# One planned kernel, planned anew: a lower rate for GpSimd's one-tile operations beside VectorE

## The chip, the core and the metric

The kernel runs on one core of a Trainium2 chip. A core has five engines that work side by side, each through its own list of instructions, in order: TensorE (PE in the profile; its weight loads are PEld), VectorE (DVE), ScalarE (ACT), GpSimd (POOL) and SyncE (SP), which here only starts transfers. They meet at semaphores. Tiles lie in SBUF, matmul results in the eight banks of PSUM. The metric is the device time of one execution in microseconds (us), and the median of several executions is compared.

## The reference, cut to what matters

```python
def _attn_ref(q, k, v, n_global, n_local):      # q, k, v: 4 x 8 heads x 768 x 64
    scores = scale * np.matmul(q, k.transpose(0, 1, 3, 2))
    keep = is_global | is_local                 # 8 first keys, and 96 keys back
    scores = np.where(keep, scores + bias, -1000000000.0)
    a = np.exp(scores - np.max(scores, axis=-1, keepdims=True))
    return np.matmul(a / (np.sum(a, axis=-1, keepdims=True) + 1e-09), v)

def _moe_ref(x, w_in, g_ln, w_sg, b_sg, w_out): # x: 4 x 768 x 512
    h = gelu(x @ w_in)
    u, v = h[..., :512], h[..., 512:]
    v_n = (v - mu) / np.sqrt(var + 1e-06) * g_ln
    v_s = np.einsum('ts,bsd->btd', w_sg, v_n) + b_sg[None, :, None]
    return x + (u * v_s) @ w_out
```

The output of the attention, heads side by side, is the x of the second part.

## The kernel before

**The work.** The attention is cut into 48 units, one for each of 4 batches, 3 pairs of query tiles (u) and 4 pairs of heads (j). A unit loads qk and v, makes its scores on PE (`score`, tile s_ps, L1049), and goes through `softmax`: DVE adds the bias and finds the row extreme (four instructions p, pst <- s_ps, L1071), ACT takes the exponential and its row sum (L1076), a tiny addition to the sums follows (pst, L1083 on ACT, L1085 on POOL or L1087 on DVE), DVE takes the reciprocal (L1089), and four instructions multiply p by it (L1096 on POOL, L1094 on ACT, L1099 on DVE). The first 16 units may do this last step on POOL alone; the later ones on POOL, ACT or DVE. These multiplications read one tile and write it: they are the "one-tile operations" of this document, called POOL_TS in the code. Then p is transposed: for the first 16 units on PE (`turn_full`, tps, L1157, copied to pt by ACT or DVE at L1162 and L1163), for the others by DVE in 32x32 blocks (tt, L1125) and two transfers through DRAM (far, L1133, and pt, L1137; `turn_blocks`). PE multiplies pt with v (av, L1184), and the result goes to x as a high and a low part (xh L1282, x L1294 to L1300 for the first units, L1257 and L1261 for the later ones).

The second part runs batch by batch, one batch behind the attention, on fp32 data split into a high and a low part, so that each product is three matmuls (mm_ps, L556 to L558): `v_tile` (then gelu and normalisation, then the split into z, L588 and L592), `u_tile`, `mix_tile` (y, L646 and L649, split into gt) and `out_tile` (o, L670 and L672). The last batch's last product is done in blocks (class `Blocks`, L801, with its sums at L747 and splits at L720 and L723). The weights arrive as 64-bit floats, are put together from their two words by one ACT and three DVE instructions (stage, L877 to L884) and are split too (win, wsg, wout, L887 to L889), all of this in the first third of the run.

**What sets the order.** No order is written by hand. `Plan.op` collects every operation with the engines it may run on, each with a busy time and an end, and `Plan.order` then plays the whole program forward on a model of the engines: at each step an engine takes the first operation that is ready, has its buffers and has the smallest key. The key is a due time, counted back from PE's list in `Plan.due`, plus a shift of the operation's own, read from the table `SHIFTS` (two digits for each operation). Three numbers in `RULES` say when an operation waits for a faster engine (`calm_at`), how early a load may start (`early`) and what a place on DVE is worth (`price`). The table is the result of a search made elsewhere, and `emit` writes the instructions in the order that comes out, so each engine's list is fixed before the kernel runs.

In that model an SBUF operation on DVE ("DVE_SB") and a two-tile operation on POOL ("POOL", such as a product or a difference of two tiles) keep out of each other's way: `begin` lets neither start before the other has ended (`held`). `emit` holds the POOL one to it with a wait on DVE (L524 and following). One-tile operations of POOL take part in none of this: `on_pool_ts` (L190) counts 0.05 + n/390 us for n columns, whatever DVE does meanwhile.

Where the model sees PE idle for over 0.6 us before 29 us, `keep_on` fills the gap with matmuls of zeros (`bsg` as both inputs, L505), so that the clock of PE stays up. How many is worked out from the gap in `zeros`. They are executed whatever the gap turns out to be.

Of the kernel before, what the change touches and what calls it, by code (L numbers as in the profile page):

```python
# [1652 lines left out]
```

## Time and profile before

| what | value |
|---|---|
| runs | 413.01, 413.61, 416.01 us; median 413.61 us |
| the profiled execution | 415.03 us, of which 413.3 us from its first to its last instruction (the span) |
| granted clock of PE | 0.998 of full speed |
| DVE, ACT and POOL instructions that the profile counts | 1032, 764 and 382 |

The profile's first table gives the busy time of each engine; a busy PE is one whose matmuls follow each other closely. In the tables of stretches each engine has its busy microseconds in that stretch and, in brackets, its instructions. In a timeline each row has a start, a length, the engine, the line of the kernel, the operation, output<-input, how many such instructions follow each other, and, in square brackets, how long the engine was idle before them and who ended that. In the tables of waits a row says who waited at which line for whom, then the total in us, how often, and the longest.

### The profile page before, as it was taken

The page shows a single profiled execution, that of the slowest core. Times are in us where ns is not written, and L with a number is a line of the kernel's source. Part 1 is how long each engine was busy: PE and PEld are TensorE (multiplying, and loading weights), DVE is VectorE, ACT ScalarE, POOL GpSimd, SP SyncE. Part 2 cuts the span into 40 slices and gives each one's busy share as a digit, 9 for nine tenths or more (in the row PEclk, how much of TensorE's full clock was granted, in tenths as well). Part 3 has the DMA queues.
Part 4 walks back from the last instruction along what each step waited for, and adds up shares of the span by engine and source line. Part 5 has one row for each costly group of instructions (what it writes and reads, how often), then busy time and mean ns, then how long its engine had stood idle before and what let it go on. Part 6 is the DMA issues. An engine that isn't in the chain of part 4 may idle for free.

```text
span 413.3 us, 11290 instructions
## 1 busy us (share of the span) xinstructions
PE 399.9 (97%) x3980; PEld 359.7 (87%) x3980; DVE 323.3 (78%) x1032; ACT 233.6 (57%) x764; POOL 231.3 (56%) x382
## 2 busy tenths in 40 slices
PE   8879989999999999999999999999999999999995
PEld 4667768899987888999999888989999888999994
DVE  6886899999887898986667699977667587734883
ACT  5889999776756574654155555844155233523510
POOL 3776888875954455454354156364354033899650
PEclk9999999999999999999999999999999999999999
DMA  7847665447779687757586586736575531000003
GB/s 237 311 150 228 215 214 177 132 118 252 217 248 299 205 238 217 199 150 219 165 256 178 166 281 173 227 89 214 162 235 144 149 120 38 1 2 0 2 17 143
DMA packets 50031, 70.15 MB, mean 170 GB/s; under 512 B 5808, under 2 KB 33968, under 8 KB 49968
## 3 DMA queue, kind: packets, MB, share of 16 engines
q1 hardware_dynamic: 49968, 69.36, 54.9%
q8 instruction: 33, 0.54, 0.5%
q14 instruction: 30, 0.25, 0.2%
HBM read 50.99 MB, written 18.35 MB: 168 GB/s over the span
## 4 chain that ended last, share of the span: by engine, by line
PE 59%; DVE 16%; DMA 9%; ACT 6%; SPq 3%; POOL 3%; issue 3%; DVEq 0%; POOLq 0%
PE mm_ps L556 15%; PE mm_ps L558 14%; PE mm_ps L557 14%; PE av L1184 5%; DMA pt<-far 5%; PE s_ps L1049 5%; PE mm_ps L801 4%; DMA far<-tt 3%; SPq L1133 3%; ACT p L1076 2%; POOL p L1096 2%; DVE tt L1125 2%; DVE p L1071 2%; PE tps L1157 2%; DVE z L592 1%
## 5 line engine op out<-in xcount | busy, mean ns | idle before, releaser
L1096 POOL TENSOR_SCALAR p<-p,pst 128x192 f32<-128x192 f32 (+1 forms) x179 | 90.9, 526 | 27.7 <-DVE pst L1089 24.1
L1076 ACT ACTIVATE p<-p,pst 128x192 f32<-128x192 f32 (+1 forms) x192 | 84.2, 444 | 31.4 <-DVE pst L1071 31.3
L556 PE MATMUL mm_ps<-wsg,z 128*128 128x384 f32 x192 | 65.0, 339 | 0.1
L557 PE MATMUL mm_ps<-wsg,z 128*128 128x384 f32 x192 | 64.3, 335 | 0.3 <-DVE wsg L889 0.3
L558 PE MATMUL mm_ps<-wsg,z 128*128 128x384 f32 x192 | 64.4, 336 | 0.1
L1071 DVE CUSTOM_DVE_ANT_0 p<-s_ps,bias 128x192 f32<-128x192 f32 (+1 forms) x192 | 57.1, 339 | 5.9 <-PE s_ps L1049 4.0
L1184 PEld LDWEIGHTS av<-pt,v 64*64 64x64 f32 x1408 | 41.1, 133 | 9.9 <-issue 4.1
L1184 PE MATMUL av<-pt,v 64*64 64x128 f32 (+1 forms) x1408 | 48.5, 250 | 1.2 <-DMA pt<-far 1.1
L672 POOL TENSOR_TENSOR o<-o,x 128x384 f32<-128x384 f32 x24 | 24.6, 1027 | 40.9 <-DVE o L670 21.4
L556 PE MATMUL mm_ps<-x,win 128*128 128x384 f32 x128 | 44.0, 343 | 0.0
L558 PE MATMUL mm_ps<-x,win 128*128 128x384 f32 x128 | 42.9, 335 | 0.0
L557 PE MATMUL mm_ps<-x,win 128*128 128x384 f32 x128 | 42.8, 335 | 0.0
L1049 PE MATMUL s_ps<-qk 64*64 64x192 f32 (+1 forms) x768 | 41.4, 320 | 0.0
L556 PE MATMUL mm_ps<-win,x 128*128 128x512 f32 x96 | 39.8, 415 | 0.0
L558 PE MATMUL mm_ps<-win,x 128*128 128x512 f32 x96 | 37.7, 393 | 0.0
L557 PE MATMUL mm_ps<-win,x 128*128 128x512 f32 x96 | 37.6, 392 | 0.0
L1125 DVE STREAM_TRANSPOSE tt<-p 128x384 f32<-128x384 f32 (+1 forms) x64 | 33.0, 542 | 5.8 <-DMA far<-tt 4.5
L556 PEld LDWEIGHTS mm_ps<-wsg,z 128*128 128x128 f32 x192 | 36.0, 188 | 1.6 <-issue 1.0
L1076 ACT ACTIVATION_READ_ACCUMULATOR p<-p,pst 128x1 f32 x192 | 37.2, 194 | 0.0
L558 PEld LDWEIGHTS mm_ps<-wsg,z 128*128 128x128 f32 x192 | 36.0, 188 | 0.8 <-DVE z L592 0.7
L557 PEld LDWEIGHTS mm_ps<-wsg,z 128*128 128x128 f32 x192 | 36.0, 188 | 0.6 <-DVE wsg L889 0.6
L1085 POOL TENSOR_SCALAR pst<-pst 128x4 f32<-128x4 f32 x39 | 9.5, 245 | 45.9 <-ACT p L1076 36.7
(130 smaller groups left out, 931.3 us busy)
## 6 DMA issues: line engine op xcount, KB each, us to landing
qk<-in_qk_in_dram SPq DMA_DIRECT2D x32, 416.0 KB, 4.2
far<-tt SPq DMA_DIRECT2D x96, 96.0 KB, 3.0
pt<-far SPq DMA_DIRECT2D x24, 384.0 KB, 4.7
v<-in_v_in_dram SPq DMA_DIRECT2D x32, 256.0 KB, 3.9
out_dram<-o SPq DMA_DIRECT2D x32, 192.0 KB, 2.2
qk<-in_qk_in_dram SPq DMA_DIRECT2D x16, 288.0 KB, 3.9
v<-in_v_in_dram SPq DMA_DIRECT2D x16, 192.0 KB, 3.1
far<-tt SPq DMA_DIRECT2D x32, 80.0 KB, 2.5
```

Of the source, the lines that this page charges most:

```text
L556: mm(ps.ap, ah, bh, start=(i == 0), stop=False)
L557: mm(ps.ap, ah, bl, start=False, stop=False)
L558: mm(ps.ap, al, bh, start=False, stop=(i == n - 1))
L672: lo = lambda eng: eng.tensor_tensor(o.ap, o.ap, xm[:, 1, :].bitcast(F32), ALU.add)
L801: mm(ps.ap, pa(h)[:, ms], pb(g), start=(first and k == n == 0), stop=True, skip_group_check=True)
L1049: nc.tensor.matmul(to, qk[rows, qc:qc + HQ], keys, start=True, stop=True)
L1071: nc.vector.tensor_tensor_reduce(out=p[:, g, 0:nk], in0=s_ps[h][:, i * W:i * W + nk], in1=bias[:, 2 * j + h, w0:w0 + nk], op0=ALU.add, op1 ...
L1076: op([on_act(nk, 0.225) + (lambda p=p, g=g, nk=nk, i=i: nc.scalar.activation(p[:, g, 0:nk], p[:, g, 0:nk], AF.Exp, bias=st[:, 0, i, g:g + ...
L1096: op([on_pool_ts(nk, -0.10) + (partial(scaled, lambda o, a, c: nc.gpsimd.tensor_scalar(o, a, c, 1.0, ALU.mult, ALU.mult)),),][:1 if n < TU ...
L1125: nc.vector.transpose(out, src.rearrange("p g (b j) -> p g b j", j=QB))
L1133: nc.sync.dma_start(far[:, :, a, 0:nt * QB].rearrange("b j f -> j b f"), tt[a * QB:(a + 1) * QB, :, 0:nt * QB])
L1184: nc.tensor.matmul(to, v[rows, vc:vc + D], of, stop=True, skip_group_check=True, **kw)
```

## The change

The model gets a rate for one-tile operations of POOL beside SBUF operations of DVE. Such an operation is counted as lengthened by 0.52 us for each us that DVE is still busy with SBUF operations, up to 1/(1 - 0.52) of its length; if DVE starts one while POOL is at work, what is left of POOL's operation is lengthened after the fact, with the operations and buffers that wait for it. PE's transposes are counted as 0.105 us for each 128 columns instead of 0.11. The search is made again on this model, so the three numbers of `RULES` and the whole table are new.

```diff
-RULES = (11.346722742318088, 16.818843568250852, 0.2893491302086273)
+RULES = (7.773165816547267, 15.003852384881524, 0.25509251116156784)
 SHIFTS = (
-    "Txi8VrTSOERgRRRKSLTBYGSjQYWsSpUpRBTgRPTfUlVPUDRPbKJ5V4YeT7YpSPS0XaNOVlSXS2c4ZEVlZVVHNVYISoRxZTTBPFOf"
...
+    "PrTKTwRJU3QHTgU5ULTpX8QFVATPSxORQsPgVgTyS2VOUuTkRrRuT6QgW6TpUiV9RTQVRURdReSISLUJUBWOT2Q1SMOCVPQARaVb"
...
-TURN = 0.11
+TURN = 0.105
...
+SLOWED = 0.52
...
-        self.ways = [(w[0].split("_")[0], w[1], w[2], w[0] in ("DVE_SB", "POOL"), w[-1])
-                     for w in ways]
+        self.ways = [(w[0].split("_")[0], w[1], w[2], w[0] in ("DVE_SB", "POOL"),
+                      w[0] == "POOL_TS", w[-1]) for w in ways]
...
+def beside(work, held):
+
+    return min(work / (1.0 - SLOWED), work + SLOWED * held) if held > 0.0 else work
...
+                if way[4]:
+                    more = beside(way[1], held["DVE"] - o.begin) - way[1]
+                    slowed = o
+                elif way[3] and e == "DVE" and slowed and free["POOL"] > o.begin:
+                    left = free["POOL"] - o.begin
+                    later = beside(left, way[1]) - left
+                    free["POOL"] += later
+                    slowed.end += later
+                    for x in slowed.after:
+                        x.ready = max(x.ready, slowed.end + SYNC)
...
                 if way[3]:
                     held[e] = free[e]
+                if e == "POOL" and not way[4]:
+                    slowed = None
```

The 24 lines that this adds shift all later lines by up to 24 (L1096 becomes L1120). No instruction that computes is added or removed; some change their engine, and the order changes on all five. The table of what changed place, counted over the lists of the two programs (the general path, which does not run, is alike in both):

| operation | engine before: count | after |
|---|---|---|
| z low part (L592) | DVE 19, POOL 5 | DVE 12, POOL 12 |
| y times u (L649) | DVE 17, POOL 15 | DVE 11, POOL 21 |
| gt low part (L592, L723) | DVE 18, POOL 12 | DVE 14, POOL 16 |
| win and wout low parts, 256 columns (L889) | DVE 1, POOL 15 | DVE 7, POOL 9 |
| p times 1/sum (L1094 to L1099) | ACT 9, DVE 4, POOL 179 | ACT 4, DVE 1, POOL 187 |
| sums + tiny (L1083 to L1087) | ACT 8, DVE 1, POOL 39 | ACT 5, DVE 3, POOL 40 |
| z high part (L588) | ACT 18, DVE 6 | ACT 21, DVE 3 |
| matmuls of zeros (L505) | 96, in runs of 12, 13, 9, 10, 8, 28, 16 | 104, in runs of 12, 15, 7, 10, 21, 25, 12, 2 |

PE changes between the small matmuls of the attention (64x64, L1049 and L1184) and full ones; it has 44 runs of small ones before and 42 now.

Three places are shown, with buffer numbers (a number is a buffer's own and differs between the two programs).

First ACT, at the fifth unit, whose softmax tiles are p_378, p_397 and pst_379 before and p_389, p_394 and pst_390 now; tps are the transposes of the units ahead of it. Before:

```order
L1076 ACTIVATE p_378,pst_379<-p_378,pst_379 128x192
L1076 ACTIVATE p_397,pst_379<-p_397,pst_379 128x192 x2
L1162 COPY pt_442<-tps_405 128x256
L877 ACTIVATE stage_447<-stage_293 128x512
L1076 ACTIVATE p_378,pst_379<-p_378,pst_379 128x192
L1282 COPY xh_463<-av_418 128x128
L1083 ACTIVATE pst_379<-pst_379,small_58 128x4
L1162 COPY pt_442<-tps_454 128x384
```

Now:

```order
L1100 ACTIVATE p_389,pst_390<-p_389,pst_390 128x192
L1100 ACTIVATE p_394,pst_390<-p_394,pst_390 128x192
L1100 ACTIVATE p_389,pst_390<-p_389,pst_390 128x192
L1100 ACTIVATE p_394,pst_390<-p_394,pst_390 128x192
L1107 ACTIVATE pst_390<-pst_390,small_58 128x4
L901 ACTIVATE stage_460<-stage_287 128x512
L1306 COPY xh_468<-av_426 128x128
L1306 COPY xh_468<-av_403 128x128
```

The four exponentials of the unit now follow each other, and its sums; before, a copy out of PSUM that waits for PE and a step on a weight stood ahead of the fourth.

Second DVE, from the same unit's reciprocal on, which is what POOL's four multiplications wait for (ISA with p is L1071's operation, s_ps is in PSUM). Before:

```order
L1089 RECIPROCAL pst_379<-pst_379 128x4
L1071 ISA p_466,pst_460<-s_ps_431,bias_87 128x192
L1071 ISA pst_460 128x1
L882 SCALAR_TENSOR_TENSOR stage_447<-stage_293,stage_447 128x512
L888 CAST win_310<-stage_371 128x512
L884 SCALAR_TENSOR_TENSOR stage_447<-stage_293,stage_447 128x512
L880 TENSOR_SCALAR stage_480<-stage_480 128x512
L882 SCALAR_TENSOR_TENSOR stage_480<-stage_381,stage_480 128x512
L1300 TENSOR_TENSOR x_478<-xh_463,x_478 128x256
L884 SCALAR_TENSOR_TENSOR stage_480<-stage_381,stage_480 128x512
L889 TENSOR_TENSOR win_310<-stage_447,win_310 128x512
```

Now:

```order
L1113 RECIPROCAL pst_390<-pst_390 128x4
L1324 TENSOR_TENSOR x_449<-xh_377,x_449 128x256
L904 TENSOR_SCALAR stage_460<-stage_460 128x512
L1095 ISA p_480,pst_481<-s_ps_442,bias_87 128x192
L1095 ISA pst_481 128x1
L1095 ISA p_486,pst_481<-s_ps_442,bias_87 128x192
L1095 ISA pst_481 128x1
L906 SCALAR_TENSOR_TENSOR stage_460<-stage_287,stage_460 128x512
L1095 ISA p_486,pst_481<-s_ps_439,bias_87 128x192
```

Before, eight operations of DVE on SBUF follow close behind the reciprocal, one behind the other; now operations that read s_ps in PSUM stand between them.

Third POOL, at the thirteenth unit, the first of the second batch (p_1077, p_1068, pst_1069 before, p_1075, p_1088, pst_1076 now). Before:

```order
L592 TENSOR_TENSOR z_1126<-vg_950,z_1126 128x512
L1300 TENSOR_TENSOR x_880<-xh_1141,x_880 128x256
L617 TENSOR_TENSOR rs_1193<-rs_1193,small_58 128x1
L1096 TENSOR_SCALAR p_1077<-p_1077,pst_1069 128x128
L1096 TENSOR_SCALAR p_1068<-p_1068,pst_1069 128x192 x2
L1096 TENSOR_SCALAR p_1077<-p_1077,pst_1069 128x128
L1096 TENSOR_SCALAR p_1164<-p_1164,pst_1152 128x128 x2
L1096 TENSOR_SCALAR p_1151<-p_1151,pst_1152 128x192 x2
```

Now:

```order
L616 TENSOR_TENSOR z_1120<-vg_933,z_1120 128x512
L1120 TENSOR_SCALAR p_1075<-p_1075,pst_1076 128x192
L1120 TENSOR_SCALAR p_1088<-p_1088,pst_1076 128x128
L1120 TENSOR_SCALAR p_1075<-p_1075,pst_1076 128x192
L1120 TENSOR_SCALAR p_1088<-p_1088,pst_1076 128x128
L1324 TENSOR_TENSOR x_888<-xh_1151,x_888 128x256
L641 TENSOR_TENSOR rs_1186<-rs_1186,small_58 128x1
L1324 TENSOR_TENSOR x_930<-xh_1236,x_930 128x256
L1120 TENSOR_SCALAR p_1159<-p_1159,pst_1160 128x192 x2
L1120 TENSOR_SCALAR p_1176<-p_1176,pst_1160 128x128 x2
```

The unit's four multiplications now stand ahead of the low part of x and of the normalisation's power (rs), behind which they stood.

More of the change, by code (lines that the diff above doesn't have):

```diff
@@ new lines @@
+    "UCU9R7R4TWVeNCTkZSStScU5TQSbWtVNTiSkQ7UARhOjNxWDX3PZK5ahWlazP5SsZwXQAWSoTHYLTJabLlS0S3UEWSR3YiORV1S9"
+    "RNSrUNTeSFRsUBRsTXTbSkRkRRPTRzRuWNQ4PwODVwQHTZVlULWgQrUqQqPJIcSWQmSETsSITgVfPoTHV2T5W2V5WwSnTASAPFT0"
+    "T9TISXOqShXyVRTOUbNxXTRUOySUMyQif4OZEVUcRXV8TDP6POSuSqOZaKU8PcVyUjWBZDUAUpO2TQTgRiNoSLVHSgIVS5VFWNWg"
+    "WOISCDGbM5CXUagEbHVtWXUoMyUobgaaQnJCTDUWSUN6WQS8VmOkRHP7U2VobpMzT0JDTXTmQLUSOXe6YkR2NDZnMdW5acSIalUj"
+    "XHNrWMV1SaUSbqN7SpQmHxXdOUcoRWLZTyRpTaQzUcSOLQggPZZ5aJT4jgPcHXPmO2PJSoMDPHZIaNCgduHHP0OnW2kbhJHzKZSW"
@@ new lines @@
+    "MNU5WOLILMWoVxVDOPZcTMOlWNMzHLWYSaWQQBN357TOK6iQNrPiEOUeaFU5RhcKMWOsPxVKcUVsUmROGRRfaIbQQgUxLnGKRBWP"
+    "UgaQYvWybiOjVZJBMITeX6HkcHTMRBYpXKJdQrQWXMWVWkPMX5LpSgToX3TtTdKactWvKIQzMXOaV9SdTYNFSNXwaHTXOIe3XAQt"
+    "dHTqVJSuTSP0IwWPOxOoTPcGfgZvO3e5NcSwXMThRfUrZVWITIQqTJTtMdWaT3TvWzYXPeXWNBT4SIWgKVa9Q8UkU9UCQdKwWJTk"
+    "SaTWSXOXO4W8ctbMYiRvQyTtRdK8ZHRNWVXzYkT8D0ZIUZPVZbTnS4TBX1ahTNQKQQO1TqlxTZXPNmTRQLSlLCYPXnXbRlY9WcOp"
+    "T1XhUDV9YrTiRoKkTgT4TaSAMvVCW4beYCMpJnUNTOVVNLXzL7QKOMQ4LZOkQnSGTohjX9XbS2Z5Z4NyUlUxO6XDo9ORdHOSV6R7"
@@ L105 @@
+    "VzS5P8VPRQUCKqSROlS8RdQAPVVCQASuVVS2PzQUVQNxatQORJUmMJQZQAQwZuV8RkUBQUUqVRV3ZcZ3S0M6PcTLRuMlRdNTMKSw"
+    "PVQqVEVKPeVzSkYUR4Q2U8YXRbRIUITJVAX7YSTxQuUrWHRcWySQSwS4Y9SLXZSAV6S0W6RDNwUEVlVEU1YLRHNvRXSWTLSSQlPl"
+    "QxWnXYRaQQ"
 )
@@ L362, in order @@
         wire, mode = 0.0, False
-        fetch, holder = Fetch(), {}
+        fetch, holder, slowed = Fetch(), {}, None
         held = {"DVE": 0.0, "POOL": 0.0}
@@ L455, in order @@
                     more += fetch.run(o.begin + more, o.words + 0.3, way[1], wire)
+                if way[4]:
[8 more added lines that the diff above has]
+                        x.ready = max(x.ready, slowed.end + SYNC)
+                    for b in slowed.bufs:
+                        if (b.kind and holder.get((b.kind, b.slot)) is b and
+                                places[b.kind][b.slot] is not None):
+                            places[b.kind][b.slot] = max(x.end for x in b.ops)
                 free[e] = o.begin + way[1] + more
```

91 lines of the change are left out of this document (39 added, 52 removed).

## The prediction

> **What bounds the kernel now.** The page's first two lines come first: of five engines one has next to no idle time.
>
> ```profile
> span 413.3 us, 11290 instructions
> PE 399.9 (97%) x3980; PEld 359.7 (87%) x3980; DVE 323.3 (78%) x1032; ACT 233.6 (57%) x764; POOL 231.3 (56%) x382
> ```
>
> PE leaves 413.3 - 399.9 = 13.4 us, and its work is the same before and after, so a plan can gain only there, in the matmuls of zeros, which count as busy, and in changes between small and full matmuls. Where that time lies, the table of stretches shows (I set the borders at the ends of PE's gaps; after the length come PE, PEld, DVE, ACT and POOL).
>
> ```profile
> 0.00:30.50 30.50, 25.47 (x378) 17.77 (x378) 24.23 (x101) 23.34 (x84) 19.26 (x44) 1.00 0.71 236
> 30.50:57.00 26.50, 26.41 (x429) 20.83 (x423) 21.73 (x99) 26.19 (x101) 19.21 (x40) 1.00 0.73 228
> 57.00:62.20 5.20, 3.64 (x23) 2.63 (x21) 4.98 (x20) 4.99 (x17) 5.20 (x10) 1.00 0.42 143
> 62.20:104.00 41.80, 41.67 (x357) 38.05 (x356) 41.15 (x127) 32.51 (x105) 31.52 (x46) 1.00 0.55 173
> 104.00:129.50 25.50, 24.33 (x261) 21.35 (x259) 21.23 (x72) 16.37 (x56) 17.82 (x32) 1.00 0.80 251
> 129.50:162.00 32.50, 32.18 (x368) 27.66 (x372) 28.42 (x102) 21.39 (x79) 15.43 (x28) 1.00 0.79 236
> 162.00:337.00 175.00, 174.90 (x1791) 162.47 (x1787) 133.97 (x429) 83.60 (x278) 77.78 (x143) 1.00 0.63 186
> 337.00:408.40 71.40, 71.29 (x409) 68.92 (x397) 47.10 (x93) 25.19 (x49) 45.12 (x45) 1.00 0.07 26
> 408.40:413.20 4.80, 0.00 (x0) 0.00 (x0) 0.49 (x1) 0.00 (x0) 0.00 (x0) 0.81 0.26 95
> ```
>
> From 162 to 408.4 us PE lacks 0.2 us: nothing can be gained there, only lost. The last 4.8 us are one addition and a store, in the same order now. The rest is 5.0 us in the first 30.5 (1.2 of them before the first instruction), 1.6 around the thirteenth unit, 1.2 between 104 and 129.5, and 0.3 after that. Second reading of the same table: ACT is full from 30.5 to 62.2 (26.19 of 26.50), DVE from 57 to 104 (41.15 of 41.80). So what PE gains early, these two have to follow.
>
> The waits say on whom PE was idle. The first two rows are of the whole span; the third is the first one's share up to 30.5 us.
>
> ```profile
> PE tps L1157 <- POOL p L1096: 5.3, 5, 1.6
> PE av L1184 <- DMA pt<-far: 1.1, 3, 0.5
> ...
> PE tps L1157 <- POOL p L1096: 3.7, 4, 1.5
> ```
>
> The largest wait of PE, 5.3 us, is for just the operations whose rate the change corrects. Is the rate wrong? POOL's groups kept apart by shape, the first up to 62.2 us, the second from 160 us on:
>
> ```profile
> L1096 POOL TENSOR_SCALAR p<-p,pst 128x192 f32<-128x192 f32 x44 | 25.6, 598 | 5.8 <-DVE pst L1089 3.2 <-DVE xh L1283 1.5 <-PE tps L1157 0.6
> ...
> L1096 POOL TENSOR_SCALAR p<-p,pst 128x192 f32<-128x192 f32 x73 | 33.2, 473 | 15.3 <-DVE pst L1089 15.1
> ```
>
> The code counts 0.442 us for 192 columns; late in the run they take 473 ns, early 598. The early ones run beside the weight operations:
>
> ```profile
> 22.90 0.69 DVE L882 SCALAR_TENSOR_TENSOR stage<-stage 128x512 int32<-128x512 int32 x1
> 22.92 4.73 POOL L1096 TENSOR_SCALAR p<-p,pst 128x192 f32<-128x192 f32 x4 [2.43 <-DVE pst L1089]
> 26.76 0.68 DVE L889 TENSOR_TENSOR win<-stage,win 128x512 fp32r<-128x512 f32 x1
> 57.66 4.64 POOL L1096 TENSOR_SCALAR p<-p,pst 128x128 f32<-128x128 f32 x8
> ```
>
> Four at 22.92 us take 4.73 us, 1.18 each, while DVE runs eight SBUF operations on end (the first and last are shown); eight at 57.66, of 128 and of 192 columns (the row names the first's shape), take 4.64, 0.58 each. PE's waits stand right behind:
>
> ```profile
> 26.36 0.55 PE L1157 MATMUL tps<-ident,p 128*128 128x128 f32 x3 [1.46 <-POOL p L1096]
> 27.70 0.55 PE L1157 MATMUL tps<-ident,p 128*128 128x128 f32 x3 [0.80 <-POOL p L1096]
> 60.67 0.66 PE L1157 MATMUL tps<-ident,p 128*128 128x128 f32 x4 [1.56 <-POOL p L1096]
> ```
>
> **The change, term by term.** *Fifth unit.* Its chain before starts on ACT and DVE:
>
> ```profile
> L908 ACT ACT_TABLE_LOAD x1 | 1.3, 1283 | 0.7 <-PEq L1639 0.7
> ...
> 5.82 0.83 ACT L1010 ACTIVATE bias<-dist 128x320 bf16<-128x320 bf16 x2 [3.59 <-DVE dist L988]
> ...
> 20.00 0.37 ACT L1162 COPY pt<-tps 128x256 f32<-128x256 f32 x1 [0.69 <-PE tps L1157]
> 20.96 0.67 ACT L877 ACTIVATE stage<-stage 128x512 f32<-128x512 f32 x1 [0.59 <-PE av L1184]
> 21.53 0.45 ACT L1076 ACTIVATE p<-p,pst 128x192 f32<-128x192 f32 x1
> 22.56 0.17 DVE L1089 RECIPROCAL pst<-pst 128x4 f32<-128x4 f32 x1
> ```
>
> The fourth exponential at 21.53 stood behind a copy and a weight step that together waited 1.3 us for PE. In the new order the four follow each other, so it can start when ACT fell idle, at 20.00 - 0.69 = 19.3; with the same 1.0 us from there to the reciprocal that is 20.3 instead of 22.56, 2.2 earlier. POOL's four then stand beside alternating PSUM and SBUF work of DVE: between 4 x 0.473 = 1.9 us and 4.73; I take 2.6, nearer the free end, since about half of DVE's time there reads PSUM. So p is ready some 2.2 + 2.1 = 4 us earlier, and the waits of 1.46 and 0.80 go. What is late next is ACT. Of the 51.2 us from 5.8 to 57 it is busy 23.34 + 26.19 - 1.5 (its table and one small instruction before) = 48.0, so it idles some 3, and its list up to the thirteenth unit shortens by 1.1 us (the groups' means over both lists). So the 3.7 us of PE's waits on POOL are not all to be had.
>
> *Zeros.* These are executed in any case:
>
> ```profile
> 7.12 2.29 PE L505 MATMUL tps<-bsg 128*128 128x384 bf16 x13
> 17.26 1.04 PE L505 MATMUL tps<-bsg 128*128 128x256 bf16 x8
> 21.69 1.73 PE L505 MATMUL av<-bsg 128*128 128x128 bf16 x28
> ```
>
> Without the drain of the last one (0.2 to 0.3 us) that is 0.16 us for each of 384 columns, 0.11 for 256, 0.055 for 128. Now there are 2 more of the first kind, 8 fewer of the second, 12 more of the third, and 2 of 512 columns (0.22 each, an estimate from these): 0.32 - 0.87 + 0.66 + 0.44 = +0.55 us. Up to the first full products I therefore have -3.7 + 0.55 = -3.15 at best, 0 at worst (ACT gives nothing back), and take -2.8: the end that ACT's 3 us of idle time allow.
>
> *Thirteenth unit.* Its multiplications started at 57.66 behind a power (0.55) and x's low part (0.73, mean 734 ns of three), both now behind them; 1.56 us of PE's wait against 0.55 + 0.73 of passed work. Between 0 and -1.6; I take -1.2. The two operations that fall behind are needed by a normalisation and by products several us later.
>
> *Changes between small and full matmuls.* 44 runs become 42.
>
> ```profile
> 54.71 0.39 PE L557 MATMUL mm_ps<-win,x 128*128 128x512 f32 x1
> 54.94 0.39 PE L558 MATMUL mm_ps<-win,x 128*128 128x512 f32 x1
> 55.26 0.70 PE L1184 MATMUL av<-pt,v 64*64 64x128 f32 x24
> ```
>
> From full to small the step is 0.32 us where it is 0.23 otherwise: 0.1 each way, so 2 x 0.2 = -0.4, between 0 and -0.8 if each change also costs a wait.
>
> *DVE to POOL.* Seven low parts of z, six products y and four low parts of gt move to POOL; six low parts of 256 columns go the other way.
>
> ```profile
> L592 POOL TENSOR_TENSOR z<-vg,z 128x512 fp32r<-128x512 f32 x5 | 6.4, 1287 | 3.6 <-DVE z L588 2.3 <-ACT z L588 1.3
> L592 DVE TENSOR_TENSOR z<-vg,z 128x512 fp32r<-128x512 f32 x19 | 13.4, 705 | 0.6
> ...
> L649 POOL TENSOR_TENSOR y<-y,u 128x384 f32<-128x384 f32 x15 | 15.1, 1018 | 9.1 <-DVE y L646 5.8 <-DVE pst L1089 1.9 <-POOL p L1096 1.2
> L649 DVE TENSOR_TENSOR y<-y,u 128x384 f32<-128x384 f32 x17 | 10.5, 620 | 0.4
> ```
>
> Each is 0.58 (z) or 0.40 (y; gt as y by my estimate) later done: 7 x 0.58 + 10 x 0.40 = 8.1 us of lateness. I cost it at nothing, because most stand after 160 us, where POOL is busy 77.78 of 175 us, PE lacks 0.1, and the last low parts of a batch's z are mostly on DVE in both lists. If that cover fails, it is up to 8.1. Of each two-tile operation on POOL, `emit` also adds a wait on DVE; behind it queue the next multiplications by 1/sum, and behind those the transposes: by DMA in that part, which POOL's idle 97 us cover. The Trainium skill speaks against this move: its GPSIMD Engine Reference, section 4.1, Engine selection, has elementwise work of two inputs belong on VectorE, about 2x slower on GpSimd. The rows agree, with 1287 against 705 ns and 1018 against 620; by that rule alone the move would be a loss of 8.1 us, by the rows of idle time it is free.
>
> *104 to 162 us.* The 1.2 and 0.3 us are waits for transfers and late tiles. The new list of PE has more full products ahead of the first units transposed by DMA, but DVE's list up to the 24th unit sums to the same 143.1 us (groups' means), and DVE was full up to 104. A PE that comes 4 us earlier may wait here: between -1.2 and +2.5; I take +0.6.
>
> The sum: -2.8 - 1.2 - 0.4 + 0 + 0.6 = -3.8 us. The profiled execution took 415.03 us, with 413.3 of span and 1.7 around it; it should become 411.2, with a span of 409.5. It lies 1.4 above the median of the runs shown, 413.61, as single runs here do (413.01 to 416.01), so the median goes to 409.8.
>
> **The rivals.**
>
> *It is given back to ACT and DVE.* For it: both are full in turn from 30.5 to 104 us, and DVE's work ahead of that point doesn't shrink. Against it: DVE idled 4.8 us between 30.5 and 57 because ACT held it, and ACT's list gets shorter. PE then waits for DVE's, ACT's or the transfers' tiles what it saved up to the first products: -3.8 + 2.8 = -1.0, so 412.6.
>
> *Everything is recovered.* If PE also loses the 1.2 and 0.3 us after 104 and pays nothing there, and ACT's 1.1 us count in full: -3.15 - 1.6 - 0.8 - 1.5 = -7, so 406.5. Against it: it takes an ACT without idle time.
>
> *Slower: POOL's two-tile work comes onto PE's path.* With the 8.1 us on the path and the other terms as forecast, 409.8 + 8.1 = 417.9; it ends above the time of before as soon as 3.8 of the 8.1 us, about half of the moved tiles, are waited for. For it: PE has no slack of its own after 162 us, and each two-tile operation also holds off DVE's next SBUF operation or is slowed by it. Against it: PE's list of waits over the whole span has four rows, and none names a two-tile operation of POOL. The rule of the Trainium skill's GPSIMD Engine Reference, section 4.1, Engine selection, would lead here.
>
> *The plan does not change what it is meant to.* The matmuls' order after 160 us keeps its grouping; if the early waits on POOL stay as they are, since the new rate is still off, the time is 413.6 plus 0.55 less 0.4: 413.8. I count it with the first rival.
>
> **How the numbers follow.** Forecast, with 407.5 to 412: 0.50. Given back or unchanged, 412 to 415: 0.26. Everything recovered, 404.5 to 407.5: 0.14. Slower, 415 to 421: 0.10. The range that leaves out 2 in 10: from 406.0, which keeps most of the recovered case, to 414.8, which keeps the second. One per cent, about what a measurement here can tell from no change, is 4.1 us: faster means under 409.5. That holds all of the recovered case and 0.24 of the forecast's 0.50, so 0.38; slower means over 417.7, somewhat over half of the last case, 0.06; the rest, 0.56, lies within.
>
> **What would show it.** Right: PE's row of waits for POOL's p under 2 us instead of 5.3; the mean of the 192-column multiplications up to 60 us nearer 500 than 598 ns; PE's first full product of win and x some 2.5 us earlier; the stretch from 162 us on unchanged in length. Given back: the same, but new rows of PE's waits for DVE, ACT or pt<-far of over 3 us between 57 and 162. Slower: PE idle after 162 us, with POOL's z, y or gt as the releaser. The forecast is wrong as a whole if PE's waits for POOL shrink and the first stage doesn't.

## The result, and the profile after

The changed kernel takes 412.84 us in the median (411.45 to 414.68, 22 runs). The kernel before, run beside it on the same chip, takes 415.27 us (413.01 to 416.82, 22 runs), so the ratio is 0.9941 with an interval of 0.9927 to 0.9955: 0.6 per cent faster, 2.4 us. The first three runs of before, with their median of 413.61 us, lay at the low side of what this kernel does; against those three the gain would look like 0.8 us. The profiled execution took 413.24 us, with a span of 411.5.

The page of the changed kernel, its span and the busy time of each engine:

```profile
span 411.5 us, 11298 instructions
PE 399.2 (97%) x3987; PEld 361.1 (88%) x3988; DVE 312.9 (76%) x1024; ACT 231.8 (56%) x749; POOL 245.5 (60%) x405
```

10.4 us moved from DVE's busy time, and 14.2 us came to POOL's: the two-tile operations that changed engine. PE now lacks 12.3 us of its span instead of 13.4. The table of stretches of the changed kernel, with the same borders (length, then PE, PEld, DVE, ACT, POOL, granted clock, DMA share, GB/s):

```profile
0.00:30.50 30.50, 27.48 (x393) 20.22 (x395) 24.50 (x104) 24.71 (x90) 17.63 (x47) 1.00 0.77 249
30.50:57.00 26.50, 26.50 (x425) 20.97 (x424) 21.66 (x98) 25.54 (x95) 20.53 (x44) 1.00 0.68 212
57.00:62.20 5.20, 4.31 (x56) 3.32 (x55) 5.13 (x20) 5.10 (x18) 3.82 (x7) 1.00 0.45 157
62.20:104.00 41.80, 39.67 (x310) 36.01 (x309) 40.50 (x126) 31.57 (x100) 28.89 (x43) 1.00 0.52 161
104.00:129.50 25.50, 25.50 (x274) 23.58 (x273) 22.02 (x77) 15.47 (x54) 17.34 (x31) 1.00 0.87 265
129.50:162.00 32.50, 32.40 (x374) 27.13 (x373) 27.52 (x98) 20.46 (x72) 21.15 (x37) 1.00 0.76 223
162.00:337.00 175.00, 174.52 (x1782) 162.90 (x1782) 128.90 (x426) 85.08 (x279) 87.61 (x154) 1.00 0.64 190
```

Three rows tell most of it. Up to 30.5 us PE has 27.48 us of work instead of 25.47. From 62.2 to 104 it now lacks 2.13 us, where it lacked 0.13. From 104 to 129.5 it lacks nothing, where it lacked 1.17. So a gain, a loss and a gain. The whole list of PE's waits in the changed kernel (total us, how often, longest):

```profile
PE av L1208 <- ACT pt L1186: 1.4, 2, 0.9
PE s_ps L529 <- DVE bsg L946: 1.2, 1, 1.2
PE mm_ps L582 <- DVE z L616: 1.1, 1, 1.1
PE tps L1181 <- POOL p L1120: 1.0, 3, 0.4
PE mm_ps L580 <- ACT xh L1306: 0.8, 1, 0.8
PE av L1208 <- DMA pt<-far: 0.5, 1, 0.5
PE mm_ps L582 <- DVE win L913: 0.2, 1, 0.2
```

POOL's p fell from 5.3 to 1.0 us. ACT's pt and xh and DVE's z are new, 3.3 us together. (The 1.2 us for bsg is the start before the first instruction of PE.)

The busy tables count zeros as work, so the balance is better read from how far PE has come. Each matmul of both kernels except the zeros is counted by its columns; the table has the time at which PE had done so many us of this work, out of 367.7. It is worked out from the starts of PE's matmuls in the profiled executions, with about 0.175 us for 384 columns of a full matmul, 0.11 for a transpose and 0.04 for 192 columns of a small matmul.

| work done by PE (us) | what stands there | before | changed | difference |
|---|---|---|---|---|
| 10 | just ahead of the first full product of win and x | 30.24 | 27.83 | -2.41 |
| 20 | | 41.52 | 39.90 | -1.62 |
| 40 | after the thirteenth unit | 65.55 | 63.29 | -2.26 |
| 50 | first products of wsg and z ahead | 76.73 | 75.07 | -1.66 |
| 55 | those products | 82.01 | 83.06 | +1.05 |
| 80 | | 108.47 | 108.55 | +0.08 |
| 100 | | 132.18 | 130.17 | -2.01 |
| 150 | | 185.21 | 183.69 | -1.52 |
| 240 | | 278.42 | 275.95 | -2.47 |
| 367.7 | PE's end | 407.95 | 405.48 | -2.47 |

The two kernels mix small and full matmuls differently, so at a given amount of work the difference can be some tenths off. It is exact where both have done the same matmuls, all of them; these are such places, with the start of PE's next matmul:

| both have done everything up to | before | changed | difference |
|---|---|---|---|
| the first full products and the transposes beside them | 31.75 | 30.47 | -1.28 |
| ahead of the thirteenth unit | 55.26 | 53.73 | -1.53 |
| behind it | 63.70 | 61.46 | -2.24 |
| shortly ahead of the products of wsg and z | 75.97 | 73.93 | -2.04 |
| 20 of these products | 81.21 | 82.08 | +0.87 |
| | 104.11 | 104.39 | +0.28 |
| | 133.22 | 131.47 | -1.75 |
| | 160.03 | 157.75 | -2.28 |
| | 170.48 | 168.88 | -1.60 |
| PE's end | 407.95 | 405.48 | -2.47 |

The gain at PE's end, 2.47 us, is that of the medians, 2.43. The two profiled executions as wholes differ by 1.8 only, since the last store took 0.7 us longer after PE's end this time; over all the runs below that tail lies between 5.3 and 6.5 us with the same instructions in it.

### The profile page after: what moved, and what is told of

Same layout as the page of the kernel before. It is cut to its first block, busy times and chain, and to the rows that moved or that the text cites. A ratio compares the mean times of both kernels' runs of the same rounds, so it can differ in the third digit from the quotient of the medians.

```text
span 411.5 us, 11298 instructions
## 1 busy us (share of the span) xinstructions
PE 399.2 (97%) x3987; PEld 361.1 (88%) x3988; DVE 312.9 (76%) x1024; ACT 231.8 (56%) x749; POOL 245.5 (60%) x405
## 4 chain that ended last, share of the span: by engine, by line
PE 82%; DVE 7%; ACT 6%; issue 1%; DMA 1%; POOL 1%; SPq 0%; DVEq 0%; POOLq 0%; ACTq 0%
PE mm_ps L580 22%; PE mm_ps L582 21%; PE mm_ps L581 21%; PE av L1208 7%; PE s_ps L1073 6%; PE mm_ps L825 4%; ACT p L1100 3%; DVE p L1095 1%; DMA pt<-far 1%; PE tps L1181 1%; PE s_ps L529 1%; ACT pt L1186 1%; DVE vg L643 1%; DVE stage L906 1%; POOL p L1120 1%
## 5 line engine op out<-in xcount | busy, mean ns | idle before, releaser
L1120 POOL TENSOR_SCALAR p<-p,pst 128x192 f32<-128x192 f32 (+1 forms) x187 | 88.3, 491 | 22.4 <-DVE pst L1113 20.7
L1073 PE MATMUL s_ps<-qk 64*64 64x192 f32 (+1 forms) x768 | 42.4, 324 | 0.0
```

Source lines behind the costliest of these rows:

```text
L1073: nc.tensor.matmul(to, qk[rows, qc:qc + HQ], keys, start=True, stop=True)
L1120: op([on_pool_ts(nk, -0.10) + (partial(scaled, lambda o, a, c: nc.gpsimd.tensor_scalar(o, a, c, 1.0, ALU.mult, ALU.mult)),),][:1 if n < TU ...
```

## The experiments

The first four ask what the three engines around PE are worth in the first stage. Each shortens one kind of work for part of a tile and leaves the order, the semaphores and all else alone. The last seven ask whether it is the rate that made the better plan. Ratios are to the kernel before, from runs on the same chip, where its median was 415.22 us beside the first four and 414.96 or 414.95 beside the last seven. They are estimates over all runs and differ from the quotients of the medians by up to 0.3 per cent where there are only four runs. Where PE's end is compared, it is one execution against one.

**POOL's multiplications made short, in the kernel before.** p of the first 16 units is multiplied by 1/sum in its first 16 columns only.

```diff
-                op([on_pool_ts(nk, -0.10) + (partial(scaled, lambda o, a, c: nc.gpsimd.tensor_scalar(
-                        o, a, c, 1.0, ALU.mult, ALU.mult)),),
+                op([on_pool_ts(nk, -0.10) + (partial(scaled, lambda o, a, c, m=16 if n < TURNS else nk: nc.gpsimd.tensor_scalar(
+                        o[:, 0:m], a[:, 0:m], c, 1.0, ALU.mult, ALU.mult)),),
```

> The kernel before, in its own order, with POOL's multiplication by 1/sum done on 16 of its 192 or 128 columns in the first 16 units (the other columns stay unscaled, so the output is not the reference's). It frees POOL of about 25 us up to 104 us. Theory: the 5.3 us of PE's waits for POOL's p go, but ACT (full from 30 to 62 us) and DVE (full from 62 to 104) give back part, so the whole gains 1.5 to 3.5 us against before (ratio 0.9915 to 0.9965). Rival, POOL alone held the early part: the gain is 5 us or more (ratio under 0.988). Rival, the new plan's gain has nothing to do with POOL: under 1 us (ratio over 0.9975).

Measured: 411.06 us (409.79 to 412.69, 4 runs), ratio 0.9893 (0.9826 to 0.9960). PE's end comes at 402.50 us, 5.45 earlier than before. Of this kernel, PE's waits and the group of POOL's multiplications:

```profile
PE tps L1157 <- POOL p L1096: 1.9, 4, 0.8
...
L1096 POOL TENSOR_SCALAR p<-p,pst 128x16 f32<-128x16 f32 x56 | 21.8, 408 | 7.9 <-DVE pst L1089 3.5 <-DVE xh L1283 2.3 <-PE tps L1157 1.5
```

POOL's busy time is 10.7 us shorter (220.6 instead of 231.3; about 25 were expected, but a multiplication of 16 columns still takes 281 ns in the median). DVE's own instructions take 2.9 us less beside them. PE's end comes 5.45 us earlier in this execution, which is the shortest of the four, and the medians differ by 4.2 (415.22 and 411.06). By these two figures POOL's multiplications held some 4 to 5 us of the kernel before. The theory had at most 3.5 and its rival at least 5; the interval of the ratio reaches from the one to the other, so which of the two holds is not decided.

Since the order is that of before, matmul by matmul, the trace shows where the gain comes: 2.1 us by 57 us, 3.05 by 104.6 us, 4.56 by 129.6 us. The stretch that cost the changed kernel 2.7 us takes 5.28 us here as before (73.90 to 79.18), so neither ACT nor DVE takes anything back. The last shortened multiplication starts at 76.5 us; what is gained between 104.6 and 129.6 us comes as PE's waits there for far transfers and for a weight become shorter or go.

**The same in the changed kernel.**

> The changed kernel with the same shortening of POOL's multiplications (same columns left out). Theory: its plan has already hidden POOL, PE waits only 1.0 us for p, so the whole gains at most 1 us against the changed kernel (409.5 to 410.5 us of span where that has 411.5). Rival, the counted rate is still too small and POOL still holds the plan: 2 us or more.

Measured: 410.49 us (409.96 to 410.94, 4 runs), ratio 0.9862 (0.9798 to 0.9927); PE's end at 403.50, 2.0 us before the changed kernel's. The theory falls and the rival's 2 us are there. PE's waits name POOL for 1.0 us in the changed kernel, and yet its multiplications cost 2: the time at which they end also sets when ACT, DVE and PE get their next tiles. That is a reading; no run here parts these ways.

**ACT's exponentials made short, in the changed kernel.** The exponential of the first 16 units is taken of 16 columns only, and FAR, the number that masks, is 10 instead of 1e20 so that what is left is small.

```diff
-FAR = 1.0e20
+FAR = 10.0
...
-                op([on_act(nk, 0.225) + (lambda p=p, g=g, nk=nk, i=i: nc.scalar.activation(
+                op([on_act(nk, 0.225) + (lambda p=p, g=g, nk=16 if n < TURNS else nk, i=i: nc.scalar.activation(
```

> The changed kernel with ACT's exponentials done on 16 columns in the first 16 units and the mask's constant 1e20 set to 10, so that what is left out stays finite (the output is not the reference's). It takes about 9 us off ACT up to 75 us. Theory: ACT now holds the first third, PE's waits for ACT's pt (1.4 us) and part of the fixed wait at 28 to 30 us go, and PE reaches its first long run of products (about 77 us) 1.5 to 3 us earlier; the end 1 to 2.5 us earlier. Rival, ACT is off the path and DVE alone holds it: under 0.5 us.

Measured: 412.42 us (411.42 to 412.94, 10 runs), ratio 0.9926 (0.9896 to 0.9955); PE's end at 405.02, 0.46 us before the changed kernel's. ACT's busy time is 6.6 us shorter (225.2 instead of 231.8). PE is 0.1 us earlier at 57 us, and the rest comes later, so the rival holds: ACT, busy for 25.54 of 26.50 us in the second stretch, holds next to nothing with its exponentials. Its copies and casts were left as they are.

**DVE's weight steps made short, in the changed kernel.** The three DVE steps that put a weight together work on 16 columns only.

```diff
-            a(), a(), 3, None, ALU.logical_shift_left))], [], [f])
+            a()[:, 0:16], a()[:, 0:16], 3, None, ALU.logical_shift_left))], [], [f])
...
-            a(), words()[:, :, 0], 29, a(), ALU.logical_shift_right, ALU.bitwise_or),)], [raw], [f])
+            a()[:, 0:16], words()[:, 0:16, 0], 29, a()[:, 0:16], ALU.logical_shift_right, ALU.bitwise_or),)], [raw], [f])
```

(and so the third, with the other word).

> The changed kernel with DVE's three weight steps (shift, and two that put the words together) done on 16 columns (the weights' values are not the reference's). It takes about 18 us off DVE up to 120 us and takes their load off POOL's multiplications. Theory: PE's 1.1 us wait for z and 0.8 us before it, at 77 to 82 us, come from a late DVE and go, so the end comes 2 to 3.5 us earlier. Rival, DVE's lateness is only what others hand it: under 1 us.

Measured: 409.65 us (408.82 to 411.27, 4 runs), ratio 0.9839 (0.9775 to 0.9903); PE's end at 402.92, 2.56 us before the changed kernel's. 1.7 of that are there by 33 us. POOL's 192-column multiplications of the first 62.2 us fall from a mean of 529 to 502 ns with POOL itself untouched. The stretch around 80 us stays long: 7.31 us (72.78 to 80.09) against 7.99 in the changed kernel, and PE's waits there for z and xh are still 0.8 and 0.6 us. So the theory has the size of the gain right and its place wrong: most of it comes ahead of 33 us, where shorter weight steps of DVE, shorter multiplications of POOL beside them, or both, can be the cause.

**Rate or draw?** The change joins a rate and a new search. The runs that follow part them. "Searched" means a random search over the table and the three numbers of RULES, an hour long or less, on the model named; the kernel that results differs in these numbers and, with the rate, in the model's lines that go with it:

```diff
-RULES = (11.346722742318088, 16.818843568250852, 0.2893491302086273)
+RULES = (14.43477508730714, 16.547368466894557, 0.16843608406935112)
 SHIFTS = (
-    "Txi8VrTSOERgRRRKSLTBYGSjQYWsSpUpRBTgRPTfUlVPUDRPbKJ5V4YeT7YpSPS0XaNOVlSXS2c4ZEVlZVVHNVYISoRxZTTBPFOf"
+    "KoaBfCtT7QL2Pvg45a8xRZLIIXcASpUpP5ORRPTfcQR4S8HgUWJNV0eDVRkraiceBpbnU8AkM9e5ZEE8UTUaNYaKB2SnhJmAHEOf"
...
+SLOWED = 0.52
```

Searched with the rate, from the table of before (the diff above; TURN stays at 0.11):

> The rate alone, searched: the model of the changed kernel but with 0.11 us for a transpose as before, a new short search from the table of BEFORE (so nothing of the changed kernel's table is in it). Theory (a search that knows the rate keeps PE from waiting for POOL's p): PE waits under 2 us for POOL's p over the span (5.3 before, 1.0 in the changed kernel), ratio to before between 0.986 and 0.995, like the changed kernel. Rival (the changed kernel's gain is that of its own table, one draw of a long search; the rate brings nothing by itself): ratio 0.995 to 1.005, and PE's waits for POOL's p of any size.

A second such search, with other random steps:

> The rate alone, searched from the table of BEFORE with other random steps: a second draw of what gave 0.992. Theory (the rate is what does it, whatever the draw): ratio 0.988 to 0.995 and PE's waits for POOL's p under 3 us. Rival (0.992 was a lucky draw): ratio over 0.996, with new waits of PE between 57 and 162 us.

Searched on with the rate, from the changed kernel's table:

> The changed kernel's own model, searched on for as long, from the table of AFTER: a version that could beat both. Theory (the 2.7 us that PE loses between 75 and 83 us in the changed kernel are of its order, so another order of the same model can have them back): 410.0 to 412.0 us, ratio to before 0.987 to 0.993, the stretch of work from 75 to 83 us shorter by 1 us or more. Rival (the plan of the changed kernel is at the bound that DVE and POOL set together up to 104 us): within 0.3 per cent of the changed kernel, and what is won at one place is lost at another.

Searched without the rate, from the changed kernel's table:

> No rate, searched: the model of before, an equally long search from the table of AFTER. Theory (the rate is what does it): a search that does not know the rate puts weight steps of DVE beside POOL's multiplications again, so PE waits 3 us or more for POOL's p, and the ratio to before is 0.995 to 1.005. Rival (a new draw does it, with or without the rate): ratio 0.988 to 0.995, within 0.4 per cent of the run searched with the rate, and POOL's waits do not tell them apart.

Searched without the rate, from the table of before:

> No rate, searched from the table of BEFORE for 50 minutes, as the run searched with the rate was for 55: the two differ in the rate alone. Theory (the rate is what does it): the search goes on preferring plans in which POOL multiplies beside DVE's weight steps, so PE's waits for POOL's p stay at 4 us or more and the ratio to before is 0.995 to 1.003. Rival (more search does it): ratio under 0.995 and under 1 us from the run searched with the rate (411.57 us).

And two without a search: the table of before on the model with the rate, and the changed kernel's table on the model of before.

> The rate alone, without a search: before's own table and three numbers, played on the model with the rate (0.11 us for a transpose). Theory (the rate helps only through the search, since a table is tuned to the model that it was searched on): slower than before, ratio 1.000 to 1.015, with new waits of PE of 2 us or more for other tiles than POOL's p. Rival (it is enough that due times and places know the rate): ratio 0.990 to 0.998, PE's waits for POOL's p under 3 us and no new ones.

> The changed kernel's table and three numbers played on the model of before (no rate, 0.11 us for a transpose), not searched. Theory (a table is good only on the model that it was searched on): 413.5 to 418 us, ratio 0.998 to 1.010, with two or more new waits of PE between 57 and 162 us. Rival (the table carries the order, the rate only led the search to it): ratio 0.991 to 0.996, PE's waits for POOL's p under 2 us.

| kernel | rate | searched from | median us (runs) | ratio to before | PE's wait for POOL's p | PE's work 50 to 55 takes |
|---|---|---|---|---|---|---|
| before | no | (as given) | 414.95 (28) | 1 | 5.3 | 5.28 |
| changed kernel | yes | (as given) | 412.84 (22) | 0.9941 (0.9927 to 0.9955) | 1.0 | 7.99 |
| first search | yes | before | 411.57 (7) | 0.9920 (0.9899 to 0.9941) | 2.5 | 5.58 |
| second search | yes | before | 413.35 (12) | 0.9956 (0.9935 to 0.9978) | 2.4 | 5.05 |
| third | yes | changed | 412.46 (6) | 0.9941 (0.9919 to 0.9964) | 0.2 | 7.05 |
| fourth | no | changed | 413.14 (10) | 0.9956 (0.9935 to 0.9977) | 2.1 | 5.95 |
| fifth | no | before | 411.34 (11) | 0.9907 (0.9881 to 0.9933) | 4.2 | 5.28 |
| rate, no search | yes | none | 415.37 (12) | 1.0018 (0.9996 to 1.0039) | 1.5 | 9.72 |
| table, no rate | no | none | 416.50 (12) | 1.0039 (1.0017 to 1.0061) | 2.2 | 7.62 |

The last two columns come from one execution of each kernel. Those of the first, second and third search and of the rate without a search took 414.69, 414.96, 414.11 and 417.61 us, 1.6 to 3.1 us over their medians; in the second search and in the rate without a search the clock of PE was also halved for 3.4 us, which is in the 9.72 us of the latter (numbers in the last section).

Against what was expected: the first search has the ratio of its theory, but 2.5 us of waits where under 2 were named. The second lies between its theory and its rival (0.9956 where 0.995 and 0.996 were the bounds). The third missed its 410.0 to 412.0 us and its 1 us (7.05 against 7.99 us in the stretch); its rival, within 0.3 per cent of the changed kernel, holds. The fourth has the theory's ratio, by 0.0006, without the theory's waits (2.1 us, not 3 or more); it also starts from a table that was found with the rate. The fifth has the theory's waits and the rival's ratio and time. The two without a search went as their theories said.

The theory that the rate does it falls. The lowest median was found without the rate, in the same kind of search from the same table, and what its theory named as the mark of a plan that doesn't know the rate is there too: PE's list of waits in that kernel begins

```profile
PE tps L1157 <- POOL p L1096: 4.2, 7, 1.4
PE s_ps L505 <- DVE bsg L922: 1.2, 1, 1.2
PE av L1184 <- DMA v<-in_v_in_dram: 0.5, 1, 0.5
```

and nothing else in it is over 0.4 us. Its four multiplications of the fifth unit still take twice what they do alone, while they are ahead of those of before (22.92 us, 4.73 long) by their start and their end:

```profile
22.11 3.96 POOL L1096 TENSOR_SCALAR p<-p,pst 128x192 f32<-128x192 f32 x4 [0.93 <-DVE pst L1089]
```

On the table's measure of work PE reaches 10 us at 28.38 us (30.24 before), 50 at 75.29, 55 at 80.57, 100 at 129.79 and its end at 404.89: a smaller first gain than the changed kernel's, 1.86 against 2.41, and hardly any of it given back in the middle (1.44 at 50 and at 55). Between this kernel, the first search and the changed kernel the intervals overlap, so which of the three is best is not shown; that all three beat the kernel before is. Five searches, three with the rate (0.9920, 0.9956, 0.9941) and two without (0.9956, 0.9907), spread more within each kind than between the kinds. Whether the rate helps in the mean of many searches stays open. The transposes' 0.105 us isn't needed for a gain: the first, second, fourth and fifth search have 0.11.

Neither the rate on the old table nor the new table without the rate gains anything: 1.0018 and 1.0039. The rate on the old table does take POOL's waits away, 5.3 to 1.5, and others stand in their place; the waits of PE in that kernel are

```profile
PE av L1208 <- DMA pt<-far: 2.0, 2, 1.2
PE mm_ps L580 <- ACT wsg L911: 1.7, 1, 1.7
PE tps L1181 <- POOL p L1120: 1.5, 5, 0.5
PE s_ps L529 <- DVE bsg L946: 1.2, 1, 1.2
PE mm_ps L581 <- DVE wsg L913: 1.2, 2, 0.6
PE tps L1181 <- DVE vg L602: 0.9, 1, 0.9
```

## Why the prediction was right or wrong

The time, 412.84 us, lies in the range, and within 1 per cent of before as the likeliest of the three chances said. The forecast of 409.8 was too low by 3.0 us. 1.66 of these are its base: it was put on a median of three runs, 413.61, and 22 runs give 415.27. The other 1.4 are the sum: -2.4 instead of -3.8. That it is off by so little is in part luck. By the places where both kernels have done the same matmuls, the term of the fifth unit was 1.3 us too large and that of the thirteenth 0.5, the stretch up to 104 us, put at nothing, cost 2.5, and the one up to 160 us, put at a cost, gave 2.6; the last two nearly cancel.

*What bounds the kernel*: right. In all thirteen profiled executions the span ends 5.3 to 6.5 us after PE's last matmul has started.

*The fifth unit and its waits on POOL*: right in kind, too large in what PE gets of it. The timeline of the changed kernel, ACT's and DVE's rows, then POOL's and PE's:

```profile
18.42 0.46 ACT L1100 ACTIVATE p<-p,pst 128x192 f32<-128x192 f32 x1
...
19.75 0.44 ACT L1100 ACTIVATE p<-p,pst 128x192 f32<-128x192 f32 x1
...
21.17 0.16 DVE L1113 RECIPROCAL pst<-pst 128x4 f32<-128x4 f32 x1
...
21.52 2.31 POOL L1120 TENSOR_SCALAR p<-p,pst 128x192 f32<-128x192 f32 x4 [1.62 <-DVE pst L1113]
...
28.42 0.58 PE L580 MATMUL mm_ps<-win,x 128*128 128x512 f32 x1
...
29.90 0.95 PE L1181 MATMUL tps<-ident,p 128*128 128x128 f32 x6 [0.44 <-POOL p L1120]
```

The fourth exponential starts at 19.75 instead of 21.53, the reciprocal at 21.17 (22.56 before, 20.3 forecast, since a weight step and a cast of DVE still stand ahead of it), and the four multiplications take 2.31 us (4.73 before, 2.6 forecast). The 192-column multiplications of the first 62.2 us, and those from 160 us on:

```profile
L1120 POOL TENSOR_SCALAR p<-p,pst 128x192 f32<-128x192 f32 x44 | 22.6, 529 | 5.0 <-DVE pst L1113 4.5 <-PE tps L1181 0.4
...
L1120 POOL TENSOR_SCALAR p<-p,pst 128x192 f32<-128x192 f32 x74 | 33.4, 468 | 9.3 <-DVE pst L1113 9.1
```

529 ns instead of 598, nearer 500 as forecast, and as before without neighbours late in the run. PE starts its first full product 2.44 us earlier (28.42; 30.86 before), as the sign said. But it does only three of them before it waits another 0.44 us for POOL's p, and three transposes that stood ahead of them in the kernel before now stand behind. Where both have done the same, the lead is 1.28 us right after and 1.53 ahead of the thirteenth unit, for a forecast of 2.8: the term is too large by 1.3.

*ACT as what is late next, capping the gain at its 3 us of idle time*: wrong as to what is late next. With ACT's exponentials 6.6 us shorter PE is 0.1 us earlier at 57 us, and the wait that it meets behind its first full products is for POOL. The cap itself is not refuted: at 35 us of work (58.38 us before) the three kernels with shortened work of POOL or DVE are 2.1, 2.7 and 3.1 us ahead of before, none of them by more than the 3.2 us that ACT idled before (51.2 - 48.0).

*The thirteenth unit, -1.2*: too large by 0.5. POOL's multiplications did come earlier and PE's wait of 1.56 us for them went, but PE came to the place early and met ACT:

```profile
58.25 0.50 PE L1208 MATMUL av<-pt,v 64*64 64x128 f32 x10 [0.89 <-ACT pt L1186]
```

So PE's lead grows from 1.53 us ahead of the unit to 2.24 behind it: 0.7 of the 1.2.

*62 to 104 us, costed at nothing*: the step that failed most plainly. The reading of the row was right (DVE full, so it has to follow), and the rival that has PE's gain given back names it, but the sum has no term for it. The stretch cost 2.5 us. Two rows of PE, two of DVE ahead of the second, and, last, the same low part of z in the kernel before:

```profile
77.23 0.44 PE L580 MATMUL mm_ps<-wsg,z 128*128 128x384 f32 x1 [0.83 <-ACT xh L1306]
...
82.08 0.44 PE L582 MATMUL mm_ps<-wsg,z 128*128 128x384 f32 x1 [1.11 <-DVE z L616]
...
79.16 1.29 DVE L906 SCALAR_TENSOR_TENSOR stage<-stage 128x256 int32<-128x256 int32 x3
...
81.35 0.68 DVE L616 TENSOR_TENSOR z<-vg,z 128x512 fp32r<-128x512 f32 x1
...
81.51 0.68 DVE L592 TENSOR_TENSOR z<-vg,z 128x512 fp32r<-128x512 f32 x1
```

The fifth low part of z ends at 82.03 us; in the kernel before it ended at 82.18. PE had come 2.0 us earlier, DVE not, and PE waited: 0.83 us for xh and 1.11 for z. Its lead of 2.04 us at 74 us is a lag of 0.87 at 82 us, and the work from 50 to 55 takes 7.99 us instead of 5.28. The two waits are 1.94 us of that; the rest isn't told apart. It is not DVE's amount of work that forces this: in the first search DVE is as full and ends its fifth low part at 79.75, in the fifth search at 80.62, with weight steps put behind it:

```profile
79.07 0.68 DVE L616 TENSOR_TENSOR z<-vg,z 128x512 fp32r<-128x512 f32 x1
```

(that of the first search). So it is the order of the changed kernel's table.

*104 to 162 us, +0.6*: wrong in sign, by the most. From 104 us on the changed kernel goes from a lag of 0.28 us to a lead of 2.28: three waits of before, 0.36 and 0.49 us for far transfers and 0.30 for a weight, are gone and no new one is there (25.50 of 25.50 us busy). Rows of waits account for 1.15; the rest lies in how groups of small and full matmuls stand in that stretch, which was not tried apart. It is not that PE had to come late to be spared: the kernel before with POOL's multiplications made short, in the same order as before, comes to this stretch 3.05 us early and leaves 129.6 us with 4.56, and the fifth search goes from 1.55 us at work 80 to 2.39 at 100. In these runs an early PE finds its tiles there; the prediction had it wait.

*After 162 us, 0, and fewer changes between small and full, -0.4*: together -0.2, from 2.28 us of lead to 2.47. 0.7 is lost by 169 us, where PE waits 0.48 us for a far transfer, and 0.9 comes back later. 0.6 of that is a place at 272 us of the kernel before, where matmuls of 384 columns followed each other 0.1 to 0.3 us late, behind no wait that the table shows. The term of -0.4 for the changes can't be told apart in this.

*DVE to POOL, costed at nothing*: right. None of PE's waits names a two-tile operation of POOL, though 17 of z, y and gt went there, and only 6 low parts of weights came back. It is worth nothing the other way as well: the first search has DVE 335.8 us busy and POOL 194.5, where before has 323.3 and 231.3, and is faster still. The Trainium skill's GPSIMD Engine Reference, section 4.1, Engine selection, prices such operations at about twice DVE's; the rows agree (1285 against 686 ns for z in the changed kernel), and the price is not on the path.

*The rivals*: "given back" came nearest in its number (412.6) and in its rows, 3.0 us of new waits between 57 and 104 us; it had no place for the 2.7 us that came back after 104, and its number stands on the same low base of 413.61. "Slower" has nothing for it.

## What to carry to other kernels

A wait that a profile names is worth what the next engine lets through: follow the freed time to the next operation that the same engine needs (here z behind DVE's weight steps) and compare when that one ends, before and after, since it costs the gain if it doesn't move. Compare two orders where both have done the same work: at equal times, or at an equal sum of unlike work, a lead can show that isn't there. A better figure in a planner's model and a new search are two changes; run the search again without the figure before the gain is put down to it. And put a forecast on more than three runs of the kernel before: here the median of three was off by more than half of the effect.

## What the runs showed of the hardware

POOL's one-tile operation beside DVE is not slowed in proportion to its size, as the model's rate has it, but held while instructions of DVE last, one or two in a row. Shortened to 16 columns it takes 281 ns in the median and still up to 1238: 4.4 times, where the model allows at most 2.08. The longest, at 26.93 us, runs beside 568 and 678 ns of two instructions of L889, one behind the other. Of the full ones, the longest of 192 columns takes 1371 ns. The long ones stand beside DVE's operations with two inputs in SBUF (L882, L884, L889), and some beside L880, with one (539 ns at 16 columns); beside those that read PSUM (L1071, L578) 192 columns stay at 421 to 436. The groups of both forms, of the kernel with 16 columns and of the kernel before:

```profile
L1096 POOL TENSOR_SCALAR p<-p,pst x56: 273/281/1238, 9.1 to 58.9; 128x16 f32<-128x16 f32 x56
```

```profile
L1096 POOL TENSOR_SCALAR p<-p,pst x56: 368/430/1371, 9.1 to 61.9; 128x192 f32<-128x192 f32 x44, 128x128 f32<-128x128 f32 x12
```

(minimum, median and maximum in ns; first and last start in us). The Trainium skill's SBUF — State Buffer, section Who interferes with whom, has it so: the two engines share a pair of ports that is locked for a whole instruction, and the loser is blocked, not throttled. The spread at 16 columns agrees.

In the profile of the kernel with the rate and no search, the clock of PE was halved behind two waits close together. The granted clock is the third number from the end:

```profile
74.00:79.50 5.50, 3.23 (x48) 2.22 (x47) 5.50 (x20) 4.81 (x17) 4.26 (x7) 1.00 0.28 74
79.50:83.00 3.50, 3.50 (x12) 3.50 (x13) 3.50 (x8) 2.58 (x9) 2.63 (x4) 0.56 0.76 216
83.00:88.00 5.00, 5.00 (x29) 5.00 (x29) 4.12 (x12) 1.50 (x5) 3.05 (x5) 0.97 0.53 185
```

PE waited 1.71 and 0.57 us within 3 us, and for about 3.4 us its matmuls of 384 columns then followed each other at 0.32 us instead of 0.17. The changed kernel's 0.83 and 1.11 us, 4 us apart, left the clock at 1.00. But so did the 1.46 and 0.80 us of the kernel before, though PE was busy there for only 0.55 of the 2.80 us from 24.90 to 27.70; and in the profile of the second search the clock stood at 0.50 from 28.32 to 31.73 us, behind waits of 0.77 and 0.54 us with PE busy for 2.87 of the 4.32 us ahead. So waits ahead of a halving are shown, and what decides whether it comes is not. The Trainium skill's TensorE: Matmul & The Clock Gate, section Why this matters for your kernels, warns of idle gaps of over some 3 us; here no single wait ahead of the two halvings was longer than 1.71 and 0.77 us.
